# One product of 512 columns for the high part of W_in times both parts of the reads, and one output transfer per queue for each tile of the last rows

## The chip, the cores and the metric

The kernel runs on one core of one Trainium2 chip. The metric is the device time of one execution in microseconds (us). TensorE (PE) multiplies matrices and adds up in PSUM, VectorE (DVE) and ScalarE (ACT) do the elementwise work and move PSUM to SBUF, SyncE (SP) and ACT issue the transfers (DMA). Each engine takes its own list of instructions in order, and waits on semaphores for the others.

## The reference

What is computed, cut to its core (B = H = 8, S = 512 tokens, Ns = 32 states, D = 64; 4352 rows of 512 go into a layer of 2048 hidden features):

```python
scores = scale * np.matmul(x, state.transpose(0, 1, 3, 2))
a = softmax(scores);   xread = np.matmul(a, state)             # 512 rows for each batch
scores2 = scale * np.matmul(state, x.transpose(0, 1, 3, 2))
a2 = softmax(scores2); sread = np.matmul(a2, x)                # 32 rows for each batch
x = concatenate([xread, sread], axis=2), heads side by side    # (8*544, 512)
h = x @ w_in
g = np.where(h >= 1, h, np.where(h <= -1, 0.0, (h + 1) ** 2 / 4))
out = g @ w_out
```

## The kernel before, in words

Tokens are worked off in batches: batches 0 to 7 are the 512 rows of `xread` each, and a ninth batch, number 8 (`b == B` in the code), is the 8 x 32 = 256 rows of `sread` of all batches together ("the reads"). Only this ninth batch is touched by the change, and it is the last stretch of the program, from 588.57 us on.

Every operand of a large product is kept in two parts, a high part rounded to the type that PE multiplies fast, and a low part that holds the rest; a product is then high x high + low x high + high x low, three matmuls in a row (lines 474 to 476 for the first layer, 532 to 534 for the second).

A batch runs over groups j of hidden features. For each group:

- `g1(b, j)` makes the hidden values in PSUM (`h`), and ACT and DVE turn them into `g`: `relu` (ACT, line 483), `square` (ACT, 486), `bound` (DVE, 490), then `high` (ACT, 496) and `low` (DVE, 501), which give `gh` and `gl`, the two parts of g.
- `g2(b, j)` multiplies `gh` and `gl` by W_out (`wo`) and adds up in the output accumulators `acc`.

On PE the order is g1(b, j), g2 of the group before, g1(b, j+1), g2(b, j) and so on, so that ACT and DVE have a whole g2 in which to make `gh` and `gl`.

In the ninth batch there are four groups of 512 features. A group's hidden values are 4 "quarters" of 128 features by 256 rows (`r` = 0 and 1 of each of two PSUM banks); a quarter takes 4 slices of the 512 input features (`k`), three matmuls of 256 columns each, 48 matmuls for a group. g2 of a group is 24 matmuls of 512 columns. The moving operand is the reads' two parts, `ath` and `atl` (they stand as `sath` and `satl` in the profile). They are made on DVE (lines 803 and 804) from `srT`, the transposed reads. The stationary operand is W_in itself, split into two parts by `wi_split(c)` for chunks c of 256 features (ACT, line 443, and DVE, line 444; `wj0h`, `wj0l` and so on). The tiles `wh` and `wl` have two buffers each, so chunk c + 2 is split into the buffers of chunk c and has to wait until PE has read that one for the last time. A group uses two chunks, c = 2j for quarters 0 and 1 and c = 2j + 1 for quarters 2 and 3.

At the end each of the two accumulators is copied to SBUF (the first on ACT, the second on DVE), and its 128 rows leave in four transfers of 32 rows, two on each of the queues of SP and ACT.

From batch 1 on nothing in the code sets the order of the engines by hand: a scheduler places the instructions from their dependencies and its own estimates. A pool that runs out of buffers is a dependency too, and so is a PSUM tile as a whole: while one bank of a two-bank tile is still to be read, it lets no product begin in the other bank.

Of the kernel before, what the change touches and what calls it, by code (L numbers as in the profile page):

```python
# [8 lines left out]
F32 = mybir.dt.float32  # L9
F32R = mybir.dt.float32r  # L10
# [3 lines left out]
ALU = mybir.AluOpType  # L14
# [94 lines left out]
def state_exchange_moe(  # L109
# [17 lines left out]
    nc = tc.nc  # L127
    B, P, NT, H, D = x.shape
    S = NT * P
    NS = 32  # L130
    DM = H * D
    NPR = H // 2
# [5 lines left out]
    TOK = S + NS  # L138
# [5 lines left out]
    work = ctx.enter_context(tc.tile_pool(name="work", bufs=2))  # L144
# [6 lines left out]
    def ps_acc(name):  # L151
        return ps.tile([P, DM], F32, tag="acc", bufs=4, name=name)
# [4 lines left out]
    def ps_h(name):  # L157
        if 1 not in banks:
            t = banks[0].tile([P, 2, 512], F32, tag="h", name=name)
            return [t, t[:, 0], t[:, 1]]  # L160
        return [None] + [banks[1].tile([P, 512], F32, tag="h", name=f"{name}_{i}") for i in range(2)]

    def ps_mm(name):
        return ps.tile([P, 2, 512], F32, tag="mm", bufs=1, name=name)
# [20 lines left out]
    srT = const.tile([P, NPR, B, NS], F32, name="srT")  # L185
# [6 lines left out]
    att_of = {}  # L192

    def load_xt(b):
        xt = work.tile([P, 2, NPR, S // 2], F32, tag="xt", bufs=1, name=f"xt{b}")
        for i in range(2):
            nc.sync.dma_start(out=xt[:, i], in_=xt_in[b, i])
        return xt

    def load_xn(b):  # L200
        if b:
            xn = work.tile([P, NT, H, D], F32, tag="xn", bufs=1, name=f"xn{b}")
        else:
            xn = rawp.tile([P, NT, H, D], F32, tag="raw", name=f"xn{b}")
        nc.sync.dma_start(out=xn, in_=x[b])
        return xn
# [202 lines left out]
    chunk = {}  # L409
# [31 lines left out]
    def wi_split(c):  # L441
        wh, wl = (v.rearrange("p (k f) -> p k f", f=CI) for v in split_tiles(f"wj{c}"))
        nc.scalar.copy(out=wh, in_=w32[c])
        nc.vector.tensor_tensor(out=wl, in0=w32[c], in1=wh.bitcast(F32), op=ALU.subtract)
        chunk[B, c] = wh, wl
# [5 lines left out]
    class Hidden:  # L451
# [6 lines left out]
        def product(self, i, ks=None):  # L458
            b, j = self.b, self.j
            n = n_of[b]  # L460
            per = S // n
            ah, al = att_of[b]
            nk = ah.shape[1]
            if i == 0 and (not ks or 0 in ks):
                self.h = ps_h(f"h{b}_{j}")
            hp = self.h[1 + i]
            for r in range(per):
                f = (2 * j + i) * per + r
                wh, wl = chunk[b, f // 2]
                sl = slice((f % 2) * P, (f % 2 + 1) * P)  # L470
                o = hp[:, r * n:(r + 1) * n]
                for k in ks or range(nk):
                    first, last = k == 0, k == nk - 1
                    nc.tensor.matmul(o, lhsT=wh[:, k, sl], rhs=ah[:, k], start=first, stop=False)  # L474
                    nc.tensor.matmul(o, lhsT=wl[:, k, sl], rhs=ah[:, k], start=False, stop=False)  # L475
                    nc.tensor.matmul(o, lhsT=wh[:, k, sl], rhs=al[:, k], start=False, stop=last)  # L476

        def part(self, i):
            return (self.u, self.h[0]) if i is None else (self.u[:, i], self.h[1 + i])
# [19 lines left out]
        def low(self):  # L499
            gh, gl = gs[self.b, self.j]  # L500
            nc.vector.tensor_tensor(out=gl, in0=self.u, in1=gh.bitcast(F32), op=ALU.subtract)  # L501

    def g1(b, j):
        hid = Hidden(b, j)
        for i in range(2):
            hid.product(i)
            hid.relu(i)
        hid.square()
        for i in range(2):
            hid.bound(i)  # L510
        hid.high()
        hid.low()

    def g2(b, j, part=(0, 8)):
        n = n_of[b]
        per = S // n
        nt = n // P
        if b not in acc:
            acc[b] = [ps_acc(f"acc{b}_{t}") for t in range(nt)]
        gh, gl = gs[b, j]  # L520
        last = j == NJ // per - 1
        pairs = [(i, t) for i in range(2 * per) for t in range(nt)]
        if last:
            pairs.sort(key=lambda p: p[1])
        pairs = pairs[part[0]:part[1]]
        for i, t in pairs:
            f = 2 * per * j + i
            oh, ol = wo[f // 2][:, 0, f % 2], wo[f // 2][:, 1, f % 2]
            c0 = (i % per) * n + t * P
            lh, ll = (v[:, i // per, c0:c0 + P] for v in (gh, gl))  # L530
            a = acc[b][t]
            nc.tensor.matmul(a, lhsT=lh, rhs=oh, start=f == 0, stop=False)  # L532
            nc.tensor.matmul(a, lhsT=lh, rhs=ol, start=False, stop=False)  # L533
            nc.tensor.matmul(a, lhsT=ll, rhs=oh, start=False, stop=f == NF - 1)  # L534
            if last and i == 2 * per - 1:
                store(b, t)
# [3 lines left out]
    def store(b, t):  # L540
        if t == 0:
            outs[b] = rawp.tile([P, NT, DM], F32, tag="raw", name=f"o{b}")
        o = outs[b][:, t]
        if b == B and t % 2:
            nc.vector.tensor_copy(o, acc[b][t])
        else:
            nc.scalar.copy(out=o, in_=acc[b][t])  # L547
        if b < B:
            r0 = b * TOK + t * P
            nc.scalar.dma_start(out=out[r0:r0 + P, :], in_=o)  # L550
        else:
            for i in range(4):
                r0 = (4 * t + i) * TOK + S
                (nc.sync if i % 2 else nc.scalar).dma_start(
                    out=out[r0:r0 + NS, :], in_=o[i * NS:(i + 1) * NS]
                )


# [51 lines left out]
    op = plan.op  # L610
# [77 lines left out]
    hid = {}  # L688
# [108 lines left out]

    loaded["xt", 2] = load_xt(2)
    for i, (b, j) in enumerate(steps):
        if (b, j) == (B, 0):  # L800
            sh, sl = (work.tile([P, NPR, B * NS], F32R, tag=t, name=f"s{t}") for t in ("ath", "atl"))
            src = srT.rearrange("p a b n -> p a (b n)")
            nc.vector.tensor_copy(sh, src)
            nc.vector.tensor_tensor(out=sl, in0=src, in1=sh.bitcast(F32), op=ALU.subtract)
            att_of[B] = (sh, sl)
        g1(b, j)
        if i + 1 < len(steps) and steps[i + 1][0] == B:
            for c in (2 * steps[i + 1][1], 2 * steps[i + 1][1] + 1):
                wi_split(c)
        before = steps[i - 1] if i else (0, NJ - 1)  # L810
        if b == B:
            g2(*before)
            continue
        nxt = atts[b + 1] = Attention(b + 1) if b + 1 < B and j == 0 else atts.get(b + 1)
        cut = 8 if j == 0 else 5
        g2(*before, (0, cut))
        if j == 0:
            if nxt:
                for k in (1, 0) if b == 1 else (b,):
                    atts[k].read2()  # L820
                for k in (1, 0) if b == 1 else (b,):
                    atts[k].scale2()
            halves = [
                sw_pair([(b, c), (b, c + 1)], [ps_acc(f"sw{b}_{c}_{hh}") for hh in range(2)]) for c in (1, 3)
            ]
            if nxt:
                nxt.scores()
                if b + 2 < B:
                    loaded["xt", b + 2] = load_xt(b + 2)
                loaded["xn", b + 1] = load_xn(b + 1)  # L830
            else:
                atts[b].read2()
            for split in halves:
                split()
            if nxt:
                nxt.second()
            else:
                atts[b].scale2()
        elif j == 1:
            if not nxt:  # L840
                sreadx = trade(sread.rearrange("p t b n -> p t (b n)"), "sread")
        elif j == 2 and nxt:
            nxt.first()
        elif j == 6 and not nxt:
            nc.vector.transpose(
                out=srT.rearrange("p r b n -> p (r b n)"), in_=sreadx.rearrange("p r k -> p (r k)")
            )
        elif j == 4:
            last = [(b, 7)] + ([(b + 1, 0)] if nxt else [])
            own = ps_h(f"sw{b}_5")  # L850
            split = sw_pair([(b, 5), (b, 6)], own[1:])
            both = ps_mm(f"sw{b}_7")
            split2 = sw_pair(last, [both[:, hh] for hh in range(2)], both)
            split()
            split2()
            if nxt:
                nxt.halves()
        g2(*before, (cut, 8))
# [44 lines left out]
```

## Time and profile before

| | |
|---|---|
| time, median of 3 runs | 644.75 us (644.06 to 646.1) |
| the profiled execution, its own time | 644.89 us |
| span of its trace | 643.1 us |
| mean granted TensorE clock | 0.997 |
| first matmul of g1(8, 0) begins | 588.57 us |
| last matmul begins | 638.67 us |

Times in the trace are counted from the span's start. A row of the timeline gives the start, the length, the engine, the line, the operation, what it writes and reads, and its shape; in brackets stands how long the engine had been idle and who ended it. A matmul's length runs into the next one's, since matmuls are pipelined: what one costs PE is the distance from start to start. On ACT and DVE too the next instruction can start a little before the one ahead has ended, where it doesn't need its result. A row of the windows gives a stretch, its length, the busy time of each engine, the granted clock of TensorE (1.00 is full speed), and the share and rate of the DMA.

### The profile page before, as it was taken

The numbers are of one execution on the slowest core, as the hardware profiler recorded it, in microseconds if no ns is written. First come the engines' busy times: TensorE is split into PE (matmuls) and PEld (weight loads), VectorE is DVE, ScalarE is ACT, GpSimd is POOL, SyncE is SP. The second block draws the span as 40 slices with busy tenths as digits, with TensorE's granted clock in tenths as the row PEclk, the third lists the DMA queues.
The fourth block names the chain that finished last, engine by engine and source line by source line (L and its number), as shares of the span: only waits on it lengthen the run. The fifth ranks groups of instructions, "written<-read, shape, count | busy, mean of one in ns | idle before, by whom it ended". The sixth has DMA issues, their size and how long they took to land.

```text
span 643.1 us, 10249 instructions
## 1 busy us (share of the span) xinstructions
PE 634.3 (99%) x4364; PEld 514.4 (80%) x4364; DVE 348.2 (54%) x493; ACT 353.9 (55%) x460; POOL 0.8 (0%) x7
## 2 busy tenths in 40 slices
PE   7999999999999999999999999999999999999997
PEld 6777787878787887878787887878787878788896
DVE  4999978542584338443574339433673345334431
ACT  4999865554564456444664457444654454444632
POOL 0000000000000000000000000000000000000000
PEclk9999999999999999999999999999999999999999
DMA  8986526000420006000510015000410012000101
GB/s 343 361 375 228 181 82 224 7 2 1 181 83 1 0 34 230 2 1 1 197 67 1 0 63 201 2 1 0 161 37 1 1 66 67 1 0 1 66 1 33
DMA packets 18477, 53.08 MB, mean 83 GB/s; under 512 B 2048, under 2 KB 7808, under 8 KB 15360
## 3 DMA queue, kind: packets, MB, share of 16 engines
q1 hardware_dynamic: 13488, 43.72, 18.3%
q10 hardware_dynamic: 4944, 8.72, 3.8%
q8 instruction: 34, 0.56, 0.4%
q14 instruction: 11, 0.09, 0.0%
HBM read 38.80 MB, written 13.63 MB: 82 GB/s over the span
## 4 chain that ended last, share of the span: by engine, by line
PE 96%; DVE 2%; ACT 1%; issue 0%; POOL 0%; POOLq 0%
PE acc L532 19%; PE acc L533 19%; PE acc L534 19%; PE h L474 10%; PE h L475 10%; PE h L476 10%; PE sw L421 5%; PE sr L366 1%; PE sc L253 1%; PE warmed L177 1%; ACT raw_o L586 0%; DVE z L294 0%; DVE m L273 0%; DVE zt L301 0%; DVE u L490 0%; DVE w L594 0%
## 5 line engine op out<-in xcount | busy, mean ns | idle before, releaser
L532 PE MATMUL acc<-wo,gh 128*128 128x512 f32 x544 | 212.8, 391 | 0.0
L533 PE MATMUL acc<-wo,gh 128*128 128x512 f32 x544 | 211.9, 389 | 0.0
L534 PE MATMUL acc<-wo,gl 128*128 128x512 f32 x544 | 211.6, 389 | 0.0
L483 ACT ACTIVATE u<-h,half 128x512 f32<-128x512 f32 (+1 forms) x128 | 91.6, 715 | 176.2 <-PE h L476 162.8
L490 DVE SCALAR_TENSOR_TENSOR u<-u,h 128x512 f32<-128x512 f32 (+1 forms) x128 | 86.4, 713 | 181.1 <-ACT u L486 181.0
L532 PEld LDWEIGHTS acc<-wo,gh 128*128 128x128 f32 x544 | 102.1, 188 | 24.6 <-issue 3.7
L534 PEld LDWEIGHTS acc<-wo,gl 128*128 128x128 f32 x544 | 102.1, 188 | 21.4
L533 PEld LDWEIGHTS acc<-wo,gh 128*128 128x128 f32 x544 | 102.2, 188 | 20.8
L501 DVE TENSOR_TENSOR gl<-u,gh 128x1024 fp32r<-128x1024 f32 x68 | 83.2, 1224 | 54.2 <-ACT gh L496 54.2
L496 ACT CAST gh<-u 128x1024 fp32r<-128x1024 f32 x68 | 71.4, 1051 | 65.3 <-DVE u L490 65.3
L486 ACT ACTIVATE u<-u 128x1024 f32<-128x1024 f32 x68 | 72.1, 1061 | 1.7
L421 PE MATMUL sw<-w,sb 64*32 64x256 f32 x1024 | 32.8, 383 | 2.9 <-DVE w L594 2.2
L421 PEld LDWEIGHTS sw<-w,sb 64*32 64x32 f32 x1024 | 18.4, 106 | 12.4 <-DVE u L490 2.5
L547 ACT COPY o<-acc 128x512 f32<-128x512 f32 x33 | 19.0, 584 | 12.1 <-PE acc L534 12.1
L474 PE MATMUL h<-ath,sw_3h 128*128 128x512 f32 x64 | 25.1, 393 | 0.0
L474 PE MATMUL h<-ath,sw_5h 128*128 128x512 f32 x64 | 24.9, 390 | 0.0
L475 PE MATMUL h<-ath,sw_5l 128*128 128x512 f32 x64 | 24.9, 389 | 0.0
L476 PE MATMUL h<-atl,sw_3h 128*128 128x512 f32 x64 | 24.9, 389 | 0.0
L475 PE MATMUL h<-ath,sw_3l 128*128 128x512 f32 x64 | 24.9, 389 | 0.0
L476 PE MATMUL h<-atl,sw_5h 128*128 128x512 f32 x64 | 24.9, 389 | 0.0
L474 PE MATMUL h<-ath,sw_1h 128*128 128x512 f32 x60 | 24.4, 407 | 0.4 <-DVE u L490 0.4
L475 PE MATMUL h<-ath,sw_1l 128*128 128x512 f32 x60 | 23.4, 390 | 0.0
(158 smaller groups left out, 704.8 us busy)
## 6 DMA issues: line engine op xcount, KB each, us to landing
xt<-in_xt_dram SPq DMA_DIRECT2D x16, 512.0 KB, 5.3
raw_i<-in_moe_w_in_dram SPq DMA_DIRECT2D x8, 1024.0 KB, 6.5
raw_o<-in_moe_w_out_dram SPq DMA_DIRECT2D x8, 1024.0 KB, 11.5
xn<-in_x_dram SPq DMA_DIRECT2D x8, 1024.0 KB, 5.8
out_dram<-o ACTq DMA_DIRECT2D x32, 256.0 KB, 2.0
e_x<-e_there SPq DMA_DIRECT2D x32, 128.0 KB, 2.9
e_there<-e SPq DMA_DIRECT2D x7, 512.0 KB, 2.6
e_there<-e SPq DMA_DIRECT2D x2, 256.0 KB, 5.1
```

What stands on the lines that cost most here:

```text
L421: nc.tensor.matmul(banks[hh][pr * NS:(pr + 1) * NS, cols], lhsT=sb[rows, b, pr], rhs=w32[c][rows, pr], start=True, stop=True,)
L474: nc.tensor.matmul(o, lhsT=wh[:, k, sl], rhs=ah[:, k], start=first, stop=False)
L475: nc.tensor.matmul(o, lhsT=wl[:, k, sl], rhs=ah[:, k], start=False, stop=False)
L476: nc.tensor.matmul(o, lhsT=wh[:, k, sl], rhs=al[:, k], start=False, stop=last)
L483: nc.scalar.activation(out=u, in_=h, func=AF.Relu, scale=0.5, bias=half)
L486: nc.scalar.activation(out=self.u, in_=self.u, func=AF.Square)
L490: nc.vector.scalar_tensor_tensor(out=u, in0=u, scalar=1.0, in1=h, op0=ALU.min, op1=ALU.max)
L496: nc.scalar.copy(out=gh, in_=self.u)
L501: nc.vector.tensor_tensor(out=gl, in0=self.u, in1=gh.bitcast(F32), op=ALU.subtract)
L532: nc.tensor.matmul(a, lhsT=lh, rhs=oh, start=f == 0, stop=False)
L533: nc.tensor.matmul(a, lhsT=lh, rhs=ol, start=False, stop=False)
L534: nc.tensor.matmul(a, lhsT=ll, rhs=oh, start=False, stop=f == NF - 1)
```

## The change

For the ninth batch a class of its own, `Last`, makes the hidden values. The two parts of the reads stand side by side in one tile, `both`, as 512 columns for each slice k, so W_in's high part is multiplied by both at once: one matmul of 512 columns in place of two of 256, then one of 256 columns with W_in's low part that adds to the first 256 columns. A quarter's result fills a whole bank: the first 256 columns hold high x high + low x high, the last 256 hold high x low. ACT copies the last 256 columns to SBUF, DVE adds the first 256 to them (tile `v`), and `relu`, `square`, `bound`, `high` and `low` work on `v`, 1024 columns at a time. Quarters 0 and 1 take the two one-bank tiles of before, quarters 2 and 3 take the two banks of the tile `mm`. `both` is made two groups earlier than the tiles of before, directly after `srT`, with the columns in the order state, then batch (4 batches in each half), so that 64 rows of an output tile leave in one transfer: one on each queue in place of two.

```diff
+    class Last(Hidden):
+        def product(self, r):
+            both = att_of[B]
+            if r == 0:
+                self.v = work.tile([P, 2, S], F32, tag="z", bufs=1, name=f"v{self.j}")
+            if r % 2 == 0:
+                self.h = ps_h(f"h{B}_{self.j}")[1:] if r == 0 else ps_mm(f"h{B}_{self.j}_2")
+            o = self.h[r % 2] if r < 2 else self.h[:, r % 2]
+            f = 4 * self.j + r
+            wh, wl = chunk[B, f // 2]
+            sl = slice((f % 2) * P, (f % 2 + 1) * P)
+            n = B * NS
+            for k in range(NPR):
+                nc.tensor.matmul(
+                    o, lhsT=wh[:, k, sl], rhs=both[:, k].rearrange("p i n -> p (i n)"),
+                    start=k == 0, stop=False,
+                )
+                nc.tensor.matmul(
+                    o[:, :n], lhsT=wl[:, k, sl], rhs=both[:, k, 0], start=False, stop=k == NPR - 1
+                )
+            v = self.v[:, r // 2, r % 2 * n:(r % 2 + 1) * n]
+            nc.scalar.copy(out=v, in_=o[:, n:])
+            nc.vector.tensor_tensor(out=v, in0=o[:, :n], in1=v, op=ALU.add)
+        def part(self, i):
+            return self.u, self.v
     def g1(b, j):
+        if b == B:
+            hid = Last(b, j)
+            for r in range(4):
+                hid.product(r)
+            for f in (hid.relu, hid.square, hid.bound, hid.high, hid.low):
+                f()
+            return
...
-            for i in range(4):
-                r0 = (4 * t + i) * TOK + S
+            rows = out.rearrange("(b r) d -> r b d", r=TOK)
+            for i in range(2):
                 (nc.sync if i % 2 else nc.scalar).dma_start(
-                    out=out[r0:r0 + NS, :], in_=o[i * NS:(i + 1) * NS]
+                    out=rows[S + i * NS // 2:S + (i + 1) * NS // 2, 4 * t:4 * t + 4],
+                    in_=o[i * P // 2:(i + 1) * P // 2],
                 )
...
-        if (b, j) == (B, 0):
-            sh, sl = (work.tile([P, NPR, B * NS], F32R, tag=t, name=f"s{t}") for t in ("ath", "atl"))
-            src = srT.rearrange("p a b n -> p a (b n)")
-            nc.vector.tensor_copy(sh, src)
-            nc.vector.tensor_tensor(out=sl, in0=src, in1=sh.bitcast(F32), op=ALU.subtract)
...
+            both = work.tile([P, NPR, 2, B * NS], F32R, tag="xt", bufs=1, name="both")
+            for t in range(2):
+                src = srT[:, :, t * 4:(t + 1) * 4]
+                sh, sl = (
+                    both[:, :, i, t * P:(t + 1) * P].rearrange("p r (n c) -> p r c n", n=NS) for i in range(2)
+                )
+                nc.vector.tensor_copy(sh, src)
+                nc.vector.tensor_tensor(out=sl, in0=src, in1=sh.bitcast(F32), op=ALU.subtract)
```

The scheduler orders the ninth batch anew. In the rows below, `h_3_1` is a hidden tile of group 3, `gh_2` the high part of group 2, `wj6h` the high part of chunk 6; the number at a name's end counts tiles. A wait names the engine that is waited for.

PE, the end of g1(8, 3) before: the last quarter's products, then g2(8, 2) in one piece.

```order
L474 MATMUL h_3_1_5209<-sath,wj7h 128x256
L475 MATMUL h_3_1_5209<-sath,wj7l 128x256
L476 MATMUL h_3_1_5209<-satl,wj7h 128x256
L532 MATMUL acc_0_5089<-wo_606,gh_2_5171 128x512 [waits Activation_49]
L533 MATMUL acc_0_5089<-wo_606,gh_2_5171 128x512
```

PE, the same place now, where the last quarter (of the tile `h_3_2`) begins:

```order
L569 MATMUL acc_0_5074<-wo_606,gh_2_5148 128x512
L570 MATMUL acc_0_5074<-wo_606,gl_2_5149 128x512
L568 MATMUL acc_1_5075<-wo_606,gh_2_5148 128x512
L518 MATMUL h_3_2_5208<-both,wj7h 128x512 [waits DVE_49]
L522 MATMUL h_3_2_5208<-both,wj7l 128x256
```

The last quarter shares a tile with the quarter before it and waits for DVE's addition from that tile. The scheduler has put 10 of the 24 matmuls of g2(8, 2) ahead of it, and 14 are left behind it. In groups 1 and 2 it is the same (10 ahead, 14 behind), in group 0 it is 8 and 16.

PE, the end of g2(8, 2) and the beginning of g2(8, 3), before:

```order
L534 MATMUL acc_1_5090<-wo_674,gl_2_5172 128x512
L532 MATMUL acc_0_5089<-wo_685,gh_3_5263 128x512 [waits Activation_49]
L533 MATMUL acc_0_5089<-wo_685,gh_3_5263 128x512
L534 MATMUL acc_0_5089<-wo_685,gl_3_5264 128x512 [waits DVE_49]
L532 MATMUL acc_0_5089<-wo_685,gh_3_5263 128x512
```

PE, the same place now:

```order
L570 MATMUL acc_1_5075<-wo_674,gl_2_5149 128x512
L568 MATMUL acc_0_5074<-wo_685,gh_3_5232 128x512 [waits Activation_49]
L569 MATMUL acc_0_5074<-wo_685,gh_3_5232 128x512
L568 MATMUL acc_1_5075<-wo_685,gh_3_5232 128x512
L569 MATMUL acc_1_5075<-wo_685,gh_3_5232 128x512
L570 MATMUL acc_0_5074<-wo_685,gl_3_5233 128x512 [waits DVE_49]
```

The third matmul of a g2 read `gl`; now four that read only `gh` stand ahead of the first that reads `gl`, in all four groups of the reads.

ACT, from group 2's `relu` on, before:

```order
L483 ACTIVATE u_2_5115<-h_2_0_5116,half 128x512 [waits DVE_49,PE_49]
L443 CAST wj6h<-w_6_99 128x1024
L483 ACTIVATE u_2_5115<-h_2_1_5117,half 128x512 [waits PE_49]
L443 CAST wj7h<-w_7_100 128x1024
L486 ACTIVATE u_2_5115<-u_2_5115 128x1024 [waits Activation_49]
L496 CAST gh_2_5171<-u_2_5115 128x1024 [waits DVE_49,Activation_49]
```

ACT now, from group 1's `square` on:

```order
L486 ACTIVATE u_1_5014<-u_1_5014 128x1024 [waits Activation_49]
L443 CAST wj6h<-w_6_99 128x1024 [waits PE_49]
L496 CAST gh_1_5062<-u_1_5014 128x1024 [waits DVE_49]
L526 COPY v_5101<-h_2_0_5102 128x256
L526 COPY v_5101<-h_2_1_5103 128x256 [waits PE_49]
L526 COPY v_5101<-h_2_2_5124 128x256 [waits PE_49]
L443 CAST wj7h<-w_7_100 128x1024 [waits PE_49]
L526 COPY v_5101<-h_2_2_5124 128x256 [waits DVE_49,PE_49]
L483 ACTIVATE u_2_5100<-v_5101,half 128x1024 [waits DVE_49]
```

The split of chunk 6 stood behind `gh` of group 1; now it stands ahead of it, and waits for PE. The split of chunk 7 stood behind the last `relu` of its group; now it stands ahead of the copy of the last quarter. In group 0 the splits of chunks 4 and 3 stand in the same two places.

DVE, group 1, before:

```order
L490 SCALAR_TENSOR_TENSOR u_1_5021<-u_1_5021,h_1_0_5022 128x512 [waits DVE_49,Activation_49]
L490 SCALAR_TENSOR_TENSOR u_1_5021<-u_1_5021,h_1_1_5023 128x512 [waits PE_49]
L501 TENSOR_TENSOR gl_1_5078<-u_1_5021,gh_1_5077 128x1024 [waits Activation_49]
L444 TENSOR_TENSOR wj6l<-w_6_99,wj6h 128x1024 [waits PE_49,Activation_49]
L444 TENSOR_TENSOR wj7l<-w_7_100,wj7h 128x1024 [waits PE_49,Activation_49]
```

DVE, group 1, now:

```order
L527 TENSOR_TENSOR v_5015<-h_1_2_5038,v_5015 128x256 [waits Activation_49]
L490 SCALAR_TENSOR_TENSOR u_1_5014<-u_1_5014,v_5015 128x1024 [waits DVE_49,Activation_49]
L444 TENSOR_TENSOR wj6l<-w_6_99,wj6h 128x1024 [waits PE_49,Activation_49]
L501 TENSOR_TENSOR gl_1_5063<-u_1_5014,gh_1_5062 128x1024 [waits Activation_49]
L527 TENSOR_TENSOR v_5101<-h_2_0_5102,v_5101 128x256 [waits Activation_49]
```

The low part of chunk 6 stood behind `gl` of group 1, and stands ahead of it now.

More of the change, by code (lines that the diff above doesn't have):

```diff
@@ L799, in state_exchange_moe @@
     for i, (b, j) in enumerate(steps):
-        if (b, j) == (B, 0):
-            sh, sl = (work.tile([P, NPR, B * NS], F32R, tag=t, name=f"s{t}") for t in ("ath", "atl"))
-            src = srT.rearrange("p a b n -> p a (b n)")
-            nc.vector.tensor_copy(sh, src)
-            nc.vector.tensor_tensor(out=sl, in0=src, in1=sh.bitcast(F32), op=ALU.subtract)
-            att_of[B] = (sh, sl)
         g1(b, j)
@@ L847, in state_exchange_moe @@
             )
+            both = work.tile([P, NPR, 2, B * NS], F32R, tag="xt", bufs=1, name="both")
[6 more added lines that the diff above has]
+                nc.vector.tensor_tensor(out=sl, in0=src, in1=sh.bitcast(F32), op=ALU.subtract)
+            att_of[B] = both
         elif j == 4:
```

## The prediction

> **What bounds the kernel now.** I read the page first, for the bound of the whole.
>
> ```profile
> span 643.1 us, 10249 instructions
> PE 634.3 (99%) x4364; PEld 514.4 (80%) x4364; DVE 348.2 (54%) x493; ACT 353.9 (55%) x460; POOL 0.8 (0%) x7
> PE 96%; DVE 2%; ACT 1%; issue 0%; POOL 0%; POOLq 0%
> ```
>
> PE is busy 99% of the span and holds 96% of the chain that ended last. So a matmul taken away is time gained, if ACT and DVE still deliver in time. Whether they do is read from the timeline of the last group.
>
> ```profile
> 622.23 0.28 PE L474 MATMUL h<-sath,wj6h 128*128 128x256 f32 x1
> ...
> 627.87 0.28 PE L476 MATMUL h<-satl,wj7h 128*128 128x256 f32 x1
> 627.99 0.40 PE L532 MATMUL acc<-wo,gh 128*128 128x512 f32 x1
> ...
> 633.45 0.39 PE L532 MATMUL acc<-wo,gh 128*128 128x512 f32 x1
> ...
> 633.91 0.39 PE L534 MATMUL acc<-wo,gl 128*128 128x512 f32 x1
> ...
> 638.67 0.39 PE L534 MATMUL acc<-wo,gl 128*128 128x512 f32 x1
> 628.19 0.69 ACT L483 ACTIVATE u<-h,half 128x512 f32<-128x512 f32 x1 [2.19 <-PE h L476]
> 628.91 1.06 ACT L486 ACTIVATE u<-u 128x1024 f32<-128x1024 f32 x1
> 630.00 1.29 DVE L490 SCALAR_TENSOR_TENSOR u<-u,h 128x512 f32<-128x512 f32 x2 [6.55 <-ACT u L486]
> 631.37 1.05 ACT L496 CAST gh<-u 128x1024 fp32r<-128x1024 f32 x1 [1.41 <-DVE u L490]
> 632.46 1.23 DVE L501 TENSOR_TENSOR gl<-u,gh 128x1024 fp32r<-128x1024 f32 x1 [1.17 <-ACT gh L496]
> ```
>
> The 48 products of g1(8, 3) take 627.99 - 622.23 = 5.76 us, 0.12 each. The 24 of g2(8, 2) take 633.45 - 627.99 = 5.46, 0.2275 each. PE never waits here, yet with little to spare: gh ends at 632.42 and is wanted at 633.45 (1.03 spare), gl ends at 633.69 and is wanted at 633.91 (0.22 spare). That chain is what the change lengthens.
>
> **The gain.** A step (one quarter, one k) was 3 x 0.12 = 0.36 and becomes 0.2275 + 0.12 = 0.3475: **0.0125 less in each of 4 groups x 4 quarters x 4 slices = 64 steps: 0.8 us**. Doubling the columns from 256 to 512 adds 0.1075, so 0.0125 of each matmul doesn't depend on its columns, and one such piece goes per step. No row shows a 512 followed by a 256 in one bank; the bounds are 0.36 (no gain) and 3 x 0.1075 = 0.3225, the columns alone (2.4 us gained). I take the sum of the two rows, since both kinds of matmul show the same fixed piece. The Trainium skill ("TensorE: Matmul & The Clock Gate", section "Back-to-back issue gap") gives N/2.4 + 2.5 ns for a lone matmul, 109 and 216 ns here; by it the gain would be 0.0025 x 64 = 0.16 us. The rows above, 120 and 227.5, differ, and they decide.
>
> **Prices of the new work.**
>
> ```profile
> L490 DVE SCALAR_TENSOR_TENSOR u<-u,h 128x1024 f32<-128x1024 f32 x8 | 9.7, 1211 | 0.6 <-ACT u L486 0.5
> L547 ACT COPY o<-acc 128x512 f32<-128x512 f32 x33 | 19.0, 584 | 12.1 <-PE acc L534 12.1
> L435 ACT CAST sw_7h<-sw 128x1024 fp32r<-128x1024 f32 x7 | 7.2, 1028 | 0.0
> L437 DVE TENSOR_TENSOR sw_1l<-sw,sw_1h 128x512 fp32r<-128x512 f32 x15 | 9.7, 686 | 9.7 <-ACT sw_1h L435 9.7
> L273 DVE TENSOR_REDUCE m<-z 128x8 f32<-128x256 f32 x4 | 1.4, 390 | 0.0
> 617.55 1.04 ACT L443 CAST wj7h<-w 128x1024 fp32r<-128x1024 f32 x1
> 618.49 1.06 ACT L486 ACTIVATE u<-u 128x1024 f32<-128x1024 f32 x1
> 618.63 1.23 DVE L444 TENSOR_TENSOR wj7l<-w,wj7h 128x1024 fp32r<-128x1024 f32 x1 [1.66 <-ACT wj7h L443]
> 619.77 1.28 DVE L490 SCALAR_TENSOR_TENSOR u<-u,h 128x512 f32<-128x512 f32 x2
> 25.10 1.22 DVE L490 SCALAR_TENSOR_TENSOR u<-u,h 128x1024 f32<-128x1024 f32 x1 [0.27 <-ACT u L486]
> 26.38 0.50 PE L474 MATMUL h<-ath,sw_1h 128*128 128x512 f32 x1 [0.40 <-DVE u L490]
> 26.71 0.40 PE L475 MATMUL h<-ath,sw_1l 128*128 128x512 f32 x1
> ```
>
> ACT's copy of 256 columns has no row: 512 take 0.584, 512 more add 0.444 (1028 - 584), so 256 less give 0.37; bounds 0.29 (half) and 0.584. DVE's addition of 256: 0.41, a little over the reduction of 256 (0.39); bounds 0.34 and 0.686. An engine takes its next independent instruction 0.94 (ACT) or 1.14 (DVE) after a split's start. A result is used 0.03 to 0.08 after its end, ACT's first use of a product comes 0.20 after the next product could start (628.19 against 627.99). After a real stall PE restarts 0.06 after the result (26.38 against 25.10 + 1.22), and the first matmul costs 0.33 in place of 0.2275: 0.1 more.
>
> **The waits it adds**, by the order of the instructions shown with the change. *Group 3*, from the moment E when its last quarter is through PE: copy 0.20 to 0.57, addition 0.60 to 1.01, relu to 2.10 (1.06, now from SBUF), square to 3.19, bound to 4.43, high to 5.56, low to 6.83. Queued behind it on PE are 14 matmuls of g2(8, 2), 3.19 us (before it was all 24). gh is usable at 5.61: **stall 2.4**, restart 0.1. Four matmuls later, at 6.62, gl is wanted, usable at 6.88: 0.26, restart 0.1. **Together 2.9.**
>
> *Group 2*: ACT splits chunk 7 ahead of the last copy, once PE has read chunk 5 (E + 0.08): cast to 1.12, copy 1.02 to 1.39, and DVE's low part 1.16 to 2.39 ahead of the addition, 2.30 to 2.71; then high to 7.26, low to 8.53. PE has 3.19 + three quarters of 1.39 = 7.36 of other work: gh is just in time, gl (wanted 8.27, usable 8.58) costs 0.31 + 0.1. **Together 0.4.**
>
> *Groups 0 and 1*: the split of chunk 4 (6) stands ahead of gh, and waits until the next group's second quarter has read chunk 2 (4) for the last time. From that quarter's end F: cast 0.08 to 1.12, high 1.02 to 2.07. PE has one quarter (1.39) left ahead of the g2: stall 0.73, restart 0.1. DVE's low part of the chunk 1.16 to 2.39, gl 2.30 to 3.53, wanted 3.13: 0.45 + 0.1. **1.4 each, 2.8 for two.** This hangs on PE's own progress, so the prices of the copies don't move it: `bound` is done long before (E + 6.1 in group 1, as in group 2, where F is E + 3.19 + 2 x 1.39 = E + 5.97 and high begins at F + 1.02).
>
> The wait of the last quarter for the addition is covered: 8 or 10 matmuls (1.8 or 2.3 us) stand ahead of it, the addition comes 1.7 after in group 0 (a split lies between on both engines) and 1.0 in group 3. With prices near the upper bounds it shows, about 0.4 in each group.
>
> Sum of waits 2.9 + 0.4 + 2.8 = 6.1 us.
>
> **The clock.** PE's stalls aren't only idle time.
>
> ```profile
> PE sw L421 <- DVE w L594: 2.2, 1, 2.2
> 14.00:14.20 0.20, 0.20 (x8) 0.15 (x16) 0.20 (x1) 0.20 (x1) 0.00 (x0) 0.65 1.07 451
> 17.40:17.60 0.20, 0.20 (x4) 0.20 (x3) 0.20 (x2) 0.00 (x0) 0.00 (x0) 0.82 0.68 287
> 24.29:27.70 3.41, 2.41 (x24) 1.59 (x25) 3.14 (x4) 3.41 (x5) 0.00 (x0) 1.00 1.00 401
> ```
>
> The one wait of 2.2 us in this trace, at the start, is followed by a half clock: 0.65 in the mean over 14.00 to 14.20 puts the drop at 14.06, 0.82 over 17.40 to 17.60 the return at 17.47, so 3.41 us at half speed, 1.7 us lost. One us of idle in 3.41 (24.29 to 27.70) left it at 1.00. The stall of 2.4 + 0.26 lies beyond the first row, but can be cut in two by the border of whatever stretch the chip counts in. 24 matmuls (5.46 us) still follow, so a drop costs its 1.7, a little less if it begins inside the stall: **1.6**. The short stalls (1.2 us in a group) lie near the row that did nothing: 0.
>
> **Small terms.**
>
> ```profile
> 543.86 0.68 DVE L803 CAST sath<-srT 128x1024 fp32r<-128x1024 f32 x1
> 544.58 1.22 DVE L804 TENSOR_TENSOR satl<-srT,sath 128x1024 fp32r<-128x1024 f32 x1
> 545.73 1.22 DVE L501 TENSOR_TENSOR gl<-u,gh 128x1024 fp32r<-128x1024 f32 x1
> 549.26 0.39 PE L534 MATMUL acc<-wo,gl 128*128 128x512 f32 x1
> L554 SPq DMA_DIRECT2D out_dram<-o x4: 315/378/422, 637.0 to 640.2; - x4
> out_dram<-o ACTq DMA_DIRECT2D x4, 64.0 KB, 2.0
> out_dram<-o ACTq DMA_DIRECT2D x32, 256.0 KB, 2.0
> ```
>
> Making `both` costs two casts (0.34 to 0.69 each, written with gaps) and two subtractions of 512 (0.68) for 1.9 us before, at most 0.8 more; the gl behind it ends at 546.95 and is wanted at 549.26: hidden. In the tail, behind DVE's copy of the last accumulator, a queue now issues one transfer in place of two: an issue takes 0.378 on SP, the last one began at 640.2, and 64 and 256 KB land alike, in 2.0 us, so a larger transfer should land no later. Gain 0 to 0.4, and I take 0.3, nearer to the rows.
>
> **Sum**: 644.89 - 0.8 + 6.1 - 0.3 = 649.9 without the clock, **651.5 with it**. The profiled execution is 0.14 above the median shown, so I say 651.4.
>
> **Rivals.**
> - *The clock holds* in the last stall: 649.8. For it, the border can split the stall. The Trainium skill ("TensorE: Matmul & The Clock Gate", section "Why this matters for your kernels") sees a drop only from idle gaps of about 3 us on; by that rule the clock holds. The 2.2 us above speak against it.
> - *No waits*: ACT and DVE deliver in time, and the gain alone is left, 643.7. For it, PE waits nowhere in the ninth batch before; against it, 0.22 of spare.
> - *Faster*: the pair costs its columns alone, 0.3225, because the fixed piece of each matmul is work on the weights that hides under the 512 columns ahead; and the waits are hidden: 644.89 - 2.4 - 0.3 = 642.2. It passes the mark of 0.3% (1.93 us, about what a measurement can tell from no change) from a pair of 0.3345 down. Both have to hold at once, and since PE waits for gh and gl, most of what it gains would be waited away.
> - *Dear copies*: 256 columns cost as 512 do. That adds 0.5 in each of groups 2 and 3 and 0.4 for the last quarter in each group, 2.6: 654.
>
> **Chances**: forecast 0.64, clock holds 0.22, no waits 0.04, faster 0.02, dear copies 0.08. So faster 0.02, same 0.04, slower 0.94. The range runs from the clock's rival with copies at their lower bounds and cheaper pairs (0.3 + 0.6 less) to the forecast with half of the dear copies and a later drop: 648.9 to 653.4.
>
> **What would show it.** Right: in the waits, PE idle for ACT's `gh` about 2.4 us once and 0.7 to 0.8 twice, and for `gl` three or four times under 0.5; L518 and L522 together 0.3475 from start to start; the granted clock at half over some 3.4 us in the last 6. Wrong: last quarters that wait for DVE (dear copies); gh in time in group 3, which would mean that 14 matmuls cover it; a pair far from 0.3475; an uncut clock.

## The result, and the profile after

The changed kernel takes **652.01 us** (median of 4 runs, 650.41 to 652.43) against 644.94 before (median of 4 runs): a ratio of 1.0104, 95% interval 1.008 to 1.0128. It is slower by 1%. The profiled execution takes 652.43 us. First the page of the changed kernel: its head, busy times and chain.

```profile
span 650.6 us, 10134 instructions
PE 637.4 (98%) x4300; PEld 511.6 (79%) x4300; DVE 354.6 (54%) x507; ACT 358.5 (55%) x472; POOL 0.8 (0%) x7
PE 93%; DVE 3%; ACT 2%; issue 0%; POOL 0%; POOLq 0%
```

64 matmuls are gone (4364 to 4300), yet PE's share of the chain fell from 96 to 93%, and those of DVE and ACT rose by a point each: PE now waits for them. The span is 7.5 us longer. Where that arose is read from PE's timeline: the first product of the reads, the last matmul, and two groups (0 and 3) in which the distance from start to start is more than a matmul.

```profile
588.84 0.39 PE L518 MATMUL h<-both,wj0h 128*128 128x512 f32 x1
...
593.07 0.40 PE L568 MATMUL acc<-wo,gh 128*128 128x512 f32 x1
...
604.05 0.28 PE L522 MATMUL h<-both,wj3l 128*128 128x256 f32 x1
604.88 0.49 PE L568 MATMUL acc<-wo,gh 128*128 128x512 f32 x1 [0.55 <-ACT gh L496]
...
605.68 0.40 PE L569 MATMUL acc<-wo,gh 128*128 128x512 f32 x1
606.34 0.49 PE L570 MATMUL acc<-wo,gl 128*128 128x512 f32 x1 [0.26 <-DVE gl L501]
...
636.28 0.39 PE L570 MATMUL acc<-wo,gl 128*128 128x512 f32 x1
638.97 0.80 PE L568 MATMUL acc<-wo,gh 128*128 128x512 f32 x1 [2.30 <-ACT gh L496]
...
645.75 0.39 PE L570 MATMUL acc<-wo,gl 128*128 128x512 f32 x1
```

The ninth batch began 0.27 us later than before (588.84 against 588.57). From there to the last matmul it takes 56.91 us, before 50.10: **6.81 more**. From the last matmul to the span's end it is 4.85, before 4.43: **0.42 more**. Together 7.5.

The waits stand in these rows. In group 0, g2 starts 604.88 - 604.05 - 0.12 = 0.71 late for gh, and its first product with gl 606.34 - 605.68 - 0.2275 = 0.43 late. In group 3 gh is 638.97 - 636.28 - 0.2275 = **2.46** late. (The bracket gives less, since a matmul's own length runs into the wait.)

ACT and DVE from the end of group 3's last quarter on:

```profile
633.47 0.37 ACT L526 COPY v<-h 128x256 f32<-128x256 f32 x1 [3.62 <-PE h L522]
633.87 0.42 DVE L527 TENSOR_TENSOR v<-h,v 128x256 f32<-128x256 f32 x1 [2.58 <-ACT v L526]
634.33 1.15 ACT L483 ACTIVATE u<-v,half 128x1024 f32<-128x1024 f32 x1 [0.49 <-DVE v L527]
635.52 1.06 ACT L486 ACTIVATE u<-u 128x1024 f32<-128x1024 f32 x1
636.61 1.23 DVE L490 SCALAR_TENSOR_TENSOR u<-u,v 128x1024 f32<-128x1024 f32 x1 [2.31 <-ACT u L486]
637.87 1.04 ACT L496 CAST gh<-u 128x1024 fp32r<-128x1024 f32 x1 [1.29 <-DVE u L490]
638.95 1.22 DVE L501 TENSOR_TENSOR gl<-u,gh 128x1024 fp32r<-128x1024 f32 x1 [1.11 <-ACT gh L496]
```

Each row begins when the one ahead has ended. From the copy to gh's end it is 638.91 - 633.47 = 5.44 us; PE's matmul for gh starts 0.06 after it. Before, it was 4.23 from relu to gh's end (628.19 to 632.42). And the rows of group 0, where a split stands ahead of gh and gl:

```profile
601.55 1.23 DVE L490 SCALAR_TENSOR_TENSOR u<-u,v 128x1024 f32<-128x1024 f32 x1 [2.53 <-ACT u L486]
602.84 1.05 ACT L443 CAST wj4h<-w 128x1024 fp32r<-128x1024 f32 x1 [0.85 <-PE h L518]
603.79 1.04 ACT L496 CAST gh<-u 128x1024 fp32r<-128x1024 f32 x1
603.92 1.22 DVE L444 TENSOR_TENSOR wj4l<-w,wj4h 128x1024 fp32r<-128x1024 f32 x1 [1.15 <-ACT wj4h L443]
605.06 1.22 DVE L501 TENSOR_TENSOR gl<-u,gh 128x1024 fp32r<-128x1024 f32 x1
```

ACT is free, but takes chunk 4 first, and that waits 0.85 us for PE; gh, whose input from `bound` is there at 601.55 + 1.23 = 602.78, follows at once behind the split, at 603.79. Last, the granted clock at the end, by windows (the number ahead of the last two is the clock):

```profile
638.00:639.00 1.00, 0.03 (x1) 0.03 (x1) 0.05 (x1) 0.92 (x1) 0.00 (x0) 0.85 0.00 0
639.00:642.00 3.00, 3.00 (x7) 2.42 (x8) 1.17 (x1) 0.00 (x0) 0.00 (x0) 0.50 0.00 0
642.00:643.00 1.00, 1.00 (x5) 0.78 (x5) 0.00 (x0) 0.00 (x0) 0.00 (x0) 0.95 0.00 0
```

A mean of 0.85 puts the drop at 638.70, while PE still waited; 0.95 puts the return at 642.10. So 3.4 us at half speed, as at the program's start.

### The profile page after: what moved, and what is told of

It is laid out like the page before. It is cut to its first block, busy times and chain, and to the rows that moved or that the text cites. A ratio compares the mean times of both kernels' runs of the same rounds, so it can differ in the third digit from the quotient of the medians.

```text
span 650.6 us, 10134 instructions
## 1 busy us (share of the span) xinstructions
PE 637.4 (98%) x4300; PEld 511.6 (79%) x4300; DVE 354.6 (54%) x507; ACT 358.5 (55%) x472; POOL 0.8 (0%) x7
## 4 chain that ended last, share of the span: by engine, by line
PE 93%; DVE 3%; ACT 2%; issue 0%; POOL 0%; POOLq 0%
PE acc L568 19%; PE acc L570 19%; PE acc L569 19%; PE h L474 9%; PE h L476 9%; PE h L475 9%; PE sw L421 4%; PE h L518 2%; PE sr L366 1%; PE sc L253 1%; PE warmed L177 1%; PE h L522 1%; DVE u L490 1%; DVE gl L501 1%; ACT u L483 1%; ACT u L486 0%
## 5 line engine op out<-in xcount | busy, mean ns | idle before, releaser
L490 DVE SCALAR_TENSOR_TENSOR u<-u,h 128x512 f32<-128x512 f32 (+1 forms) x120 | 81.3, 716 | 173.7 <-ACT u L486 173.6
L483 ACT ACTIVATE u<-h,half 128x512 f32<-128x512 f32 (+1 forms) x120 | 86.3, 719 | 158.7 <-PE h L476 147.5
```

The lines of the kernel that those rows point to most:

```text
L483: nc.scalar.activation(out=u, in_=h, func=AF.Relu, scale=0.5, bias=half)
L490: nc.vector.scalar_tensor_tensor(out=u, in0=u, scalar=1.0, in1=h, op0=ALU.min, op1=ALU.max)
```

## The experiments

Two accounts of the waits stood against each other. *Shared tile*: the last quarter has to wait for its neighbour's tile, so the scheduler moved 10 of the 24 covering matmuls ahead of it, and reordered the splits as well. *Long chain*: copy, addition and the full relu are simply too long for g2 to cover. Beside them stood the clock, and the tail (from the last matmul's start to the span's end), which had come out on the other side of the forecast.

### The last rows as before

```diff
-            rows = out.rearrange("(b r) d -> r b d", r=TOK)
-            for i in range(2):
+            for i in range(4):
+                r0 = (4 * t + i) * TOK + S
                 (nc.sync if i % 2 else nc.scalar).dma_start(
-                    out=rows[S + i * NS // 2:S + (i + 1) * NS // 2, 4 * t:4 * t + 4],
-                    in_=o[i * P // 2:(i + 1) * P // 2],
+                    out=out[r0:r0 + NS, :], in_=o[i * NS:(i + 1) * NS]
...
-                    both[:, :, i, t * P:(t + 1) * P].rearrange("p r (n c) -> p r c n", n=NS) for i in range(2)
+                    both[:, :, i, t * P:(t + 1) * P].rearrange("p r (c n) -> p r c n", n=NS) for i in range(2)
```

> The changed kernel with its last rows put back: columns of the reads by batch, then state, and four transfers of 32 rows for each tile. From the last matmul's start to the span's end it was 4.43 us before and 4.85 after. If the new transfers are what made the tail longer (by their pattern or by their size), it is 4.4 to 4.5 here, an issue takes 0.38 in place of 0.59 and lands in 1.7 to 2.0 in place of 2.4 to 2.7. If the tail is longer for another reason (the half clock, or the engines' state at the end), it stays at 4.85. The waits of PE stay: 0.7 for gh in groups 0 and 1, 2.3 to 2.5 in group 3.

Measured: one execution, 649.85 us, span 648.0, the last matmul at 643.64, so the tail is 4.36. The rows of the tile view, for the changed kernel and then for this one, give the shortest, the median and the longest issue in ns:

```profile
L590 SPq DMA_DIRECT2D out_dram<-o x2: 571/594/616, 644.5 to 646.9; - x2
```

```profile
L590 SPq DMA_DIRECT2D out_dram<-o x4: 315/376/421, 642.4 to 645.1; - x4
```

The tail's 0.4 is the new transfers'. The run held something else. Its waits are the same (2.45 for gh in group 3), but the clock stayed at 1.00 through them:

```profile
634.00:638.00 4.00, 1.70 (x9) 1.07 (x7) 1.32 (x2) 2.55 (x3) 0.00 (x0) 1.00 0.00 0
638.00:642.00 4.00, 3.93 (x16) 2.94 (x17) 1.13 (x1) 0.20 (x1) 0.00 (x0) 1.00 0.00 0
```

PE is busy only 1.70 of 4 us ahead of 638, and nothing follows. From the first product of the reads (587.77) to the last matmul it is 55.87 us, where the profiled execution of the changed kernel has 56.91. So the same wait dropped the clock in one execution and not in another, and the drop is worth 1.04 us. (There is no drop at the program's start in this run either, and the reads begin 1.07 us earlier.)

### Four transfers in the new pattern

```diff
-            for i in range(2):
+            for i in range(4):
                 (nc.sync if i % 2 else nc.scalar).dma_start(
-                    out=rows[S + i * NS // 2:S + (i + 1) * NS // 2, 4 * t:4 * t + 4],
-                    in_=o[i * P // 2:(i + 1) * P // 2],
+                    out=rows[S + i * NS // 4:S + (i + 1) * NS // 4, 4 * t:4 * t + 4],
+                    in_=o[i * P // 4:(i + 1) * P // 4],
```

> The changed kernel with four transfers of 32 rows for each tile, but in the new pattern (8 states x 4 batches each; columns by state, then batch). Theory pattern: an issue takes long because its rows go to places in the output that don't follow each other, so each of the four takes 0.5 to 0.6, two on each queue, and the tail grows to 5.0 to 5.4. Theory size: 128 KB in one transfer take longer than 64 KB, so the issue falls back to 0.38, the landing to 1.7 to 2.0, and the tail to 4.4 to 4.5.

Measured: 650.5 us once, span 648.7, last matmul at 643.57: a tail of 5.13. The tile view, SP's issues:

```profile
L590 SPq DMA_DIRECT2D out_dram<-o x4: 657/682/834, 642.3 to 645.4; - x4
```

Half the size, the same pattern, and an issue takes 0.68, longer than the 0.59 of the larger one. It is the pattern: rows that follow each other in the tile go to four batches in turn, 544 rows apart in the output. Size as the cause of the long issue is out. The tail itself tells less: over the seven traces with two transfers in this pattern it is 4.85 to 5.11, over the four traces with the old rows 4.36 to 4.43. So the new transfers cost 0.4 to 0.7 us, and the 5.13 of this run lies hardly above.

### A tile of its own for the last quarter

```diff
-            if r % 2 == 0:
-                self.h = ps_h(f"h{B}_{self.j}")[1:] if r == 0 else ps_mm(f"h{B}_{self.j}_2")
-            o = self.h[r % 2] if r < 2 else self.h[:, r % 2]
+            if r == 0:
+                self.h = ps_h(f"h{B}_{self.j}")[1:]
+            elif r == 2:
+                self.h += [
+                    ps_mm(f"h{B}_{self.j}_2")[:, 0],
+                    banks[1].tile([P, 512], F32, tag="h", name=f"h{B}_{self.j}_3"),
+                ]
+            o = self.h[r]
```

> The changed kernel, but the last quarter of a group gets a PSUM tile of its own (one bank, from the pool of quarters 0 and 1), so it no longer waits for the addition from its neighbour. Theory shared tile: the wait for that tile made the scheduler put the last quarter behind 8 or 10 matmuls of g2, and so took the cover from the chain; with a tile of its own 23 or 24 matmuls (5.3 to 5.5 us) stand behind the last quarter, against a chain of 5.6 to gh and 6.9 to gl. PE then waits 0.2 to 0.3 for gh and 0.3 for gl in group 3 and nowhere else, the clock doesn't drop, and the time is 645.0 to 646.0 with the new transfers. Theory long chain: copy, addition and the full relu (1.2 us more than before) are too long for any order; the waits stay at 4 us or more, and the time is above 648.5.

Measured: **645.66 us** (10 runs, 644.78 to 647.12) against 644.89 before (13 runs), ratio 1.0014 (1.0004 to 1.0024). PE's timeline at the start of group 3's g2, and the last matmul:

```profile
633.13 0.39 PE L575 MATMUL acc<-wo,gl 128*128 128x512 f32 x1
633.59 0.50 PE L573 MATMUL acc<-wo,gh 128*128 128x512 f32 x1
...
634.39 0.39 PE L574 MATMUL acc<-wo,gh 128*128 128x512 f32 x1
634.85 0.50 PE L575 MATMUL acc<-wo,gl 128*128 128x512 f32 x1
...
639.29 0.39 PE L575 MATMUL acc<-wo,gl 128*128 128x512 f32 x1
```

gh is 633.59 - 633.13 - 0.2275 = 0.23 late, gl 0.23 as well, and no other wait is left in the ninth batch. Of the 7.1 us that the change cost, 6.4 are gone (the drop of the clock is part of them), though copy, addition and full relu are all still there. PE's timeline has 24 matmuls behind the last quarter of group 3 here and 14 in the changed kernel: 10 x 0.2275 = 2.28 us more of cover, and the wait for gh is 2.46 - 0.23 = 2.23 shorter. The chain is too long by 0.23 for a whole g2; the rest of the wait is lost cover. The long chain as the main cause falls.

### Buffers of their own for chunks 4 and 6

```diff
-        wh, wl = (v.rearrange("p (k f) -> p k f", f=CI) for v in split_tiles(f"wj{c}"))
+        tags = {4: ("e2", "e2"), 6: ("ath", "atl")}.get(c, ("wh", "wl"))
+        wh, wl = (
+            work.tile([P, 1024], F32R, tag=t, name=f"wj{c}{s}").rearrange("p (k f) -> p k f", f=CI)
+            for t, s in zip(tags, "hl")
+        )
```

> The changed kernel, with buffers of their own for the two parts of chunks 4 and 6 (tiles that are free by then), so that their splits needn't wait for PE. Theory: the 0.75 + 0.65 us in groups 0 and 1 came from these splits standing ahead of gh and gl. Without the wait at least one of the two groups (chunk 6, group 1) loses its wait for gh, and since the scheduler orders anew, group 3's wait falls too, to about 1.4 + 0.3; the last matmul begins 2 to 3 us earlier than in the changed kernel. If the waits in groups 0 and 1 came from the chain itself (copy, addition, relu), they stay at 0.7 in both groups, and nothing is gained.

Measured: 648.32 us (4 runs). From the first product of the reads to the last matmul it is 641.90 - 588.52 = 53.38 us, 2.5 less than the 55.87 of the run with the old rows (in both the clock holds at the end). PE's waits in this kernel (total, times, longest):

```profile
PE acc L572 <- ACT gh L500: 1.7, 2, 1.2
PE acc L574 <- DVE gl L505: 0.2, 1, 0.2
```

Group 1 waits for gh no more. Group 3 waits 1.36 in place of 2.46, and that isn't the buffers' own doing: the new order leaves 19 matmuls behind the last quarter in place of 14, and 5 x 0.2275 = 1.14. Group 0 still waits 0.71. There the new order has put another split, chunk 5's, ahead of gh, and that waits for PE in the same way:

```profile
602.52 1.05 ACT L447 CAST wj5h<-w 128x1024 fp32r<-128x1024 f32 x1 [0.85 <-PE h L522]
603.48 1.04 ACT L500 CAST gh<-u 128x1024 fp32r<-128x1024 f32 x1
```

So the wait of groups 0 and 1 is that of a split ahead of gh, as forecast: it goes where none stands there.

### relu by halves, the shared tile kept

```diff
-            return self.u, self.v
+            return (self.u, self.v) if i is None else (self.u[:, i], self.v[:, i])
...
             for r in range(4):
                 hid.product(r)
+                if r % 2:
+                    hid.relu(r // 2)
-            for f in (hid.relu, hid.square, hid.bound, hid.high, hid.low):
+            for f in (hid.square, hid.bound, hid.high, hid.low):
```

> The changed kernel with a shorter chain: relu is done by halves (quarters 0 and 1, then 2 and 3), as before the change, the shared tile left as it is. Theory shared tile: the chain from the last quarter is only about 0.5 us shorter, so a wait for gh of 1.5 to 2.0 us stays in group 3, and the scheduler's new order may take the waits for gh in groups 0 and 1 away. Theory long chain: without the full relu the wait in group 3 is gone or below 0.5.

Measured: 647.67 us once. PE's timeline in group 3:

```profile
633.22 0.39 PE L572 MATMUL acc<-wo,gl 128*128 128x512 f32 x1
635.08 0.50 PE L570 MATMUL acc<-wo,gh 128*128 128x512 f32 x1 [1.48 <-ACT gh L496]
```

635.08 - 633.22 - 0.2275 = 1.63 are left in group 3, 0.83 less than in the changed kernel. The chain from the copy to gh's end is 5.02 in place of 5.44, and 16 matmuls stand behind the last quarter in place of 14 (0.46): about half of the gain is the chain's, half the cover's. Groups 0 and 1 wait for gh no more, since their splits stand behind gh here. So the shared tile alone doesn't put the splits ahead of gh; with it, the full relu does. A shorter chain helps, but doesn't give the cover back.

### The last wait filled with products

```diff
+    rest = ps_acc("rest")
+    for _ in range(10):
+        nc.tensor.matmul(rest, lhsT=gs[B, 2][0][:, 0, :P], rhs=wo[0][:, 0, 0], start=True, stop=True)
     g2(*steps[-1])
```

> The changed kernel with ten extra products of 512 columns (2.3 us, into an accumulator that nothing reads) ahead of the last g2, where PE would wait 2.4 us for gh of group 3; no result changes. Theory: the wait itself isn't shortened, so with the clock held the last matmul begins as late as in the runs in which the clock held: 55.8 to 56.0 us from the first product of the reads to the last matmul, against 56.9 in the changed kernel's profiled run and 55.9 with the old rows, where the clock held by itself. No run drops the clock at the end, and the slowest runs of the changed kernel (652.3 to 652.4) are missing: 650.0 to 651.5. If idle PE isn't what drops the clock, the half clock at the end still shows in some runs, and the time is that of the changed kernel, 652.0.

Measured: 650.83 us (4 runs, 649.95 to 652.5); 55.63 us from the first product of the reads to the last matmul, clock 1.00 at the end. 55.63 is 0.2 below what was expected, and one execution lies above the expected 651.5. The scheduler put one of the ten products earlier; nine stand in the wait, and 0.24 of it is left. That alone settles little, since the clock had held by itself in the two kernels with four transfers. So both kernels ran once more, side by side:

> The changed kernel once more, unaltered, for more executions beside those with the filled wait. Each execution has a mean granted clock: 0.996 to 0.997 with one drop of 3.4 us, 0.993 to 0.994 with two, 0.999 to 1.000 with none. Theory: the 2.5 us wait drops the clock in a good part of the executions (three in four or so, by where a period of 3.41 us cuts the wait), so several of ten show 0.993 to 0.994, and the median is 651.5 to 652.3.

> The kernel with ten extra products in the last wait once more, on the same chip and in the same rounds. Theory: no execution shows two drops (none at 0.995 or below), and the median lies 0.5 to 1.2 us below that of the unaltered kernel. If idle PE doesn't drop the clock, both kernels show the same clocks and the same median.

Measured, mean granted clock and time of every execution of both runs:

```
unaltered: 0.993 652.43, 0.994 652.35, 0.997 651.67, 0.999 650.41, 0.998 650.22, 0.993 652.37, 0.997 651.42, 0.997 651.78
filled:    0.999 650.51, 0.997 652.50, 0.997 651.14, 0.998 649.95, 0.997 651.11, 1.000 650.54, 0.997 652.74, 0.999 650.23, 0.997 651.13
```

With the wait unfilled, 3 executions of 8 lose as much clock as two drops cost, and they are the three above 652. With it filled, none of 9 does, as expected. By the counts alone this isn't settled: three such executions would all fall among these 8 of 17 by chance in one case of 12. The medians of the second pair are 651.6 and 651.11, 0.49 apart where 0.5 to 1.2 was expected, over all executions 651.7 and 651.1. Two filled executions at 652.5 and 652.7 aren't explained by their clock; they stay open. At least 3 of 8 drop the clock at the end: three more (0.997) show one drop, and a mean doesn't say where. So the expected share of three in four can't be told from this.

Why the same wait drops the clock only at times can be read from the traces. The drops of the changed kernel's first trace lie 638.70 - 14.06 = 624.64 = 183 x 3.413 us apart. The changed kernel's second trace, of the execution at 650.22, drops its clock only behind the last matmul, at 646.43 by the mean of 0.71; counted back from there in steps of 3.413, borders lie at 639.60, 636.19 and 632.78. First the stretch that ends at the drop, then the two among which this trace divides the same wait:

```profile
635.28:638.70 3.42, 1.39 (x7) 0.80 (x5) 1.23 (x1) 2.10 (x3) 0.00 (x0) 1.00 0.00 0
```

```profile
646.00:647.00 1.00, 0.00 (x0) 0.00 (x0) 0.00 (x0) 0.00 (x0) 0.00 (x0) 0.71 0.71 207
632.78:636.19 3.41, 2.55 (x12) 1.75 (x10) 1.10 (x2) 2.21 (x2) 0.00 (x0) 1.00 0.00 0
636.19:639.60 3.41, 1.90 (x7) 1.29 (x8) 1.54 (x2) 1.04 (x1) 0.00 (x0) 1.00 0.00 0
```

PE is idle for 2.03 us of the first stretch, and for 0.86 and 1.51 of the other two: there the border cuts the wait. Divided in this way, all twelve traces agree. Ahead of each of the seven drops within the program (six at its start, one in this wait) a stretch holds 1.98 to 2.20 us of idle PE; in no stretch between the clock's first rise and the last matmul that isn't followed by a drop is there more than 1.94. These sums rest on the ends of matmuls, which the profiler models, so the exact limit isn't shown; and no run was made to move the border. This trace also shows what the drop costs in one and the same kernel: from the first product of the reads to the last matmul it takes 643.33 - 587.49 = 55.84, against 56.91 with it, 1.07 less.

### What is left of the change without its waits

Own tile, relu by halves and the rows and transfers of before, all edits shown above.

> Own tile for the last quarter, relu by halves, and the rows and transfers of before: the pairs of 512 and 256 columns alone, without what they brought. Theory: the chain to gh is 5.1 us and covered by 23 or 24 matmuls, gl is 0.2 to 0.3 late once, the tail is 4.4 again, and 64 steps of 0.352 in place of 0.36 give 0.5: 644.4 to 644.8 against 644.9, no difference that can be told. If some other part of the change costs time (making both, the copies and additions on ACT and DVE), it stays above 645.5.

Measured: 644.57 us (11 runs, 643.8 to 646.6) against 644.36 (21 runs), ratio 1.0007 (0.9997 to 1.0017): no difference. From the first product of the reads to the last matmul it is 638.29 - 588.37 = 49.92 us, 0.18 less than before. A group's pairs take 5.64 in place of 5.76, 0.5 less in all; on PE's timeline about half of that goes at gl of group 3, which is still 0.15 late and costs 0.11 for the restart. The quarter's products were then put in groups:

```diff
             for k in range(NPR):
                 nc.tensor.matmul(o, lhsT=wh[:, k, sl], rhs=both[:, k].rearrange("p i n -> p (i n)"), ...)
+            for k in range(NPR):
                 nc.tensor.matmul(o[:, :n], lhsT=wl[:, k, sl], rhs=both[:, k, 0], ...)
```

> The same, with a quarter's four products of 512 columns first and its four of 256 behind them. The changed kernel's trace shows 0.235 for a 512 and 0.117 for a 256 where they take turns, 0.352 for a pair; grouped, rows of before give 0.2275 and 0.12, 0.3475. Theory turns: the 0.0045 per pair come from taking turns (a large product behind a small one waits for its weights), so 64 x 0.0045 = 0.3 us are gained on the kernel with turns. If a 512 product of this operand costs 0.235 in any order, nothing is gained.

Measured: 644.23 us (11 runs), ratio 0.9996 (0.9988 to 1.0005). The first product of group 0 and the g2 behind its four quarters, with turns and then grouped:

```profile
588.37 0.39 PE L523 MATMUL h<-both,wj0h 128*128 128x512 f32 x1
...
594.01 0.40 PE L575 MATMUL acc<-wo,gh 128*128 128x512 f32 x1
```

```profile
588.28 1.07 PE L523 MATMUL h<-both,wj0h 128*128 128x512 f32 x4
...
593.86 0.40 PE L576 MATMUL acc<-wo,gh 128*128 128x512 f32 x1
```

16 pairs take 5.64 and 5.58 us: 0.3525 and 0.349 each. Most of the 0.0045 does come from taking turns in these two traces, 0.2 us in all; in the total it can't be told.

## Why the prediction was right

Direction and size came out: 651.4 with a range of 648.9 to 653.4, measured 652.01. By its steps:

- **The gain**: 0.8 forecast. In the changed kernel 12 pairs take 593.07 - 588.84 = 4.23 us, 0.3525 each and not 0.3475, so 64 x 0.0075 = 0.5. Mis-sized: a 512 that takes turns with a 256 costs 0.235 in the mean, and no row of before showed such turns.
- **Waits of group 3**: 2.4 for gh forecast, 2.46 measured; 0.26 for gl, 0.23 in the run in which the clock held. Copy 0.37, addition 0.42, bound 1.23 as priced; relu from SBUF 1.15 in place of 1.06.
- **Waits of groups 0 and 1**: 0.73 and 0.45 forecast, 0.71 and 0.43 measured. Group 2: gl 0.23 late, forecast 0.31. The buffers show that the split ahead of gh is the cause. That it stands there is the scheduler's order for the shared tile and the full relu together: with a tile of its own, or with relu by halves, it stands behind gh.
- **Last quarters**: no wait, as forecast; dear copies are out.
- **The sum of the waits** was 6.1; from the first product of the reads to the last matmul the run with the clock held takes 55.87 - 50.10 = 5.77 more. With the gain put back (0.5) that is 6.3, where the single waits and their restarts add to 5.9; the other 0.3 is spread over matmuls next to the switches and wasn't followed.
- **The clock**: the mechanism is there, 3.4 us at half speed, but it came in 3 of 8 executions at least, where the forecast gave it more than an even chance, and it cost 1.04 to 1.07 and not 1.6. Mis-sized because the drop begins 0.27 us inside the wait, and because the wait for gl (0.23 and its restart) vanishes under the slower matmuls. What was said of the border that can cut the wait is what the second trace of the changed kernel shows, and 2.0 us of idle within one stretch were enough for a drop.
- **The tail**: 0.3 gained forecast, 0.42 lost (0.4 to 0.7 over all traces). The step that failed is "64 and 256 KB land alike, so a larger transfer should land no later": the rows priced the size, and the pattern was what cost. An issue takes 0.59 and lands in 2.4 to 2.7 us.
- **Making `both`** was hidden, as forecast: no wait in the groups behind it.

So the total is closer than its steps, and in part by luck. For the profiled execution the sum gave 651.5, and it took 652.43. The gain came out 0.3 short, the waits 0.2 longer and the tail 0.7 worse, and the ninth batch began 0.27 later, a start that lies within the 588.44 to 588.85 of the other traces with a drop of the clock at the program's start. Together that is 1.5 us, and the milder clock took 0.56 of it back: with the drop at its measured price the sum would have been 1.5 too low. The executions at 650.2 to 650.4 don't bear out the 649.8 of the rival "the clock holds", for that is reckoned from an execution with a drop at the start, and they have none (mean clock 0.998 and 0.999). In the run with the old rows the reads began 1.07 us earlier without that drop; with as much added these executions stand at about 651.4, again some 1.5 above the rival.

## What to carry to other kernels

A product that is merged at the cost of an elementwise step is priced at the place where that step is last waited for, and with the order that the scheduler makes of it: here 64 saved matmuls gave 0.5 us, and one shared PSUM tile, with an order that took the cover from a chain and put splits ahead of it, took more than ten times that. Before a merge, count what stands on PE behind the last product that feeds the chain, and give each piece of a result that is read at its own time a tile of its own.

## What the runs showed of the hardware

- A wait of PE of 2.46 us drops its clock to half for 3.4 us in some executions and not in others (3 of 8 at least, by their mean clock). In the twelve traces each drop falls on a border of stretches of 3.413 us, behind a stretch with 1.98 us or more of idle PE; stretches with 1.94 or less were followed by none.
- A transfer whose successive rows go to four batches in turn, 544 rows apart in the output, takes 0.59 us (128 KB) or 0.68 (64 KB) to issue on SP, where one of 64 KB whose rows stay together takes 0.38.
- Of two matmuls that take turns, 512 and 256 columns, the pair takes 0.3525 us, and 0.349 when four of each kind follow each other.
